# Row-wise scores for one head in four of ten groups, in an attention and Fourier kernel

## The chip, the cores and the metric

The kernel runs on one core of one Trainium2 chip. TensorE (PE) multiplies matrices into PSUM, VectorE (DVE), ScalarE (ACT) and GpSimd (POOL) work on tiles, and SyncE (SP) issues nearly all DMAs, in order, one queue for all of them. The metric is the time of one execution in microseconds on the device. Times are given as the median of several runs; the profile is of one further execution.

## The reference

Two independent parts stand side by side in the output. Part A is an attention with a compressive memory: 2,048 positions, 32 heads of 18 features, in four segments of 512 positions. In each segment a causal softmax attention runs within the segment; from the second segment on it is blended with a lookup in a memory that sums the keys and values of the segments before. Part B is a Fourier mixing layer: two products with DFT matrices, of which the real part is kept.

```python
for s in range(4):
    logits = einsum("bhqd,bhkd->bhqk", qs, ks) * 18 ** -0.5 + causal_mask
    a_dot = einsum("bhqk,bhkd->bhqd", softmax(logits), vs)
    a_mem = (phi(qs) @ M) / (phi(qs) @ z + 1e-6)
    o[s] = g * a_mem + (1 - g) * a_dot
    M, z = M + phi(ks).T @ vs, z + phi(ks).sum()
A = concat(o) @ wo
B = dft_seq_re @ (x @ dft_hid_re.T) - dft_seq_im @ (x @ dft_hid_im.T)
```

All of it is float32, and the kernel keeps its precision by splitting numbers into a high and a low part (or three bfloat16 parts) and adding the products.

## The kernel before

It has three stages. In the first (to some 220 us) the projections are computed segment by segment. Queries and keys go to DRAM scratch (`qd`, `kd`) in three bfloat16 parts each, values (`vd`, [128, 4 position blocks, 8 groups, 220]) and the finished memory lookups (`amd`, [4, 128, 576]) too. In the second, the attention of all heads and the Fourier products run interleaved. The third, short one multiplies by `wo`.

The change lies in the second stage. Its units:

- A group G is four heads of one segment; there are 32 groups, 8 for each segment. Head n is head h = n % 4 of group n // 4. `stack_load(G)` loads the group's `ks` and `qs`, `value_load(G)` its values `vst`, `memory_load(G)` its lookups into `og` (from G = 8 on).
- A phase p handles pairs of heads, an even one and the odd one next to it, at several lags, so a head passes through several phases. A phase has eight slots with nominal widths (`SLOTS`). After each slot the generator `attention` yields, DMAs and work put off by `later` are issued, and dense Fourier matmuls (`d`) are dealt out until their share of the nominal total is reached. All order is written out in this way; every engine executes its instructions in that order.
- All 512 x 512 scores of a head, in the causal lower half, are 1,280 columns of PE work: row block i (128 queries) needs (i + 1) x 128 keys.

An odd head is formed by rows. `f_fill` (kinds 0, 1, 2) multiplies the rows' scores into PSUM (`scores`, L958), and DVE masks the diagonal block and takes each row's minimum of the negated score in one pass (`smallest`, L964). `f_exp` takes the exponential on ACT with that minimum as bias (L984, L987), into `pf`. `f_split_hi` (ACT, L994) and `f_split_lo` (POOL for 768 columns, DVE for 512, L998) split it into two float16 halves `hl`. `f_turn` (L1003) transposes `hl` by a DMA into `ptt`, as `pv` needs keys on the partitions. That is lag 2 for the scores, lag 3 for split and turn, lag 4 for `pv`, which multiplies by the values (L1076, L1077).

An even head is formed transposed, without a DMA transpose. `s_fill` scores the rows at lag 0 only for their minima (`NEGM`). For both even heads of a group, `maxima` (POOL) cuts the minima into three bfloat16 parts, `maxima_transpose` turns them on PE (L1015) and two small DMAs (L1019) put them under `qs` as three more rows. At lag 3 `t_fill` computes the transposed scores with the minima folded in (seven matmuls, L1032 to L1041), and ACT takes exponentials into the high half `phi` and the full `pf` (L1044, L1045). `t_mask` zeroes the upper triangle of the diagonal blocks (POOL, L1049), `t_hi` copies (ACT, L1054), and `t_lo` makes `plo` (DVE and POOL, L1059).

PSUM has two banks for `s` tiles and two for `t` tiles, taken in turns. `pf` is a ring of three tiles; `phi`, `plo`, `hl` and `ptt` are rings of two. The dense part loads chunks `craw` four ahead (`c_load`, L441); `c_cut` splits a chunk on ACT (`chi`, L451) and POOL (`clo`, L456).

Of the kernel before, what the change touches and what calls it, by code (L numbers as in the profile page):

```python
# [23 lines left out]
P = 128  # L24
# [10 lines left out]

COPIES = ((0, 3, 2, 0), (1, 3, 2, 2), (0, 5, 1, 0), (1, 5, 1, 1))
COPY_ROWS = 144


@with_exitstack  # L40
def infini_attention_and_fnet(ctx: ExitStack, tc: tile.TileContext, xT, wqk, w8, wv, wo, beta, xtT, cT, hT, out):
# [10 lines left out]
    vd = [dram.tile([P, 4, 8, 220], BF16, name=f"vd{s}") for s in range(NSEG)]  # L52
    amd = [dram.tile([4, P, D], F32, name=f"amd{s}") for s in range(NSEG)]
# [255 lines left out]
    def project_v(s, j, meanwhile):  # L309
        xh, xl, xt = X[s]  # L310
        js = slice(j * P, (j + 1) * P)
        vs = vs_bufs[(4 * s + j) % 3]
        r = sb.tile([P, H, DH], F32, name="vr", tag="r", bufs=3)
        for h in range(2):
            cs, hs = slice(h * 288, (h + 1) * 288), slice(16 * h, 16 * h + 16)
            o = ps.tile([P, 288], F32, name="v", tag="acc", bufs=5)
            terms = []
            for k in range(4):
                terms += [(xh[k][:, js], WV[1][k][:, cs]), (xh[k][:, js], WV[0][k][:, cs]),
                          (xl[k][:, js], WV[0][k][:, cs])]  # L320
            terms += [(xt[:, js], WV[2][:, cs]), (xt[:, js], WV[3][:, cs])]
            chain(o, terms)
            o = o.rearrange("p (h d) -> p h d", d=DH)
            act.activation(vs[:, hs, 18:36], o, AF.Copy)
            if s < 3:
                split(vn[j % 2][:, 0, hs, :DH], vn[j % 2][:, 1, hs, :DH], o)
            dve.tensor_tensor(r[:, hs], o, vs[:, hs, 18:36], OP.subtract)
            if h == 0 and s < 3:
                k_natural(j)
            next(meanwhile, None)  # L330
        if s < 3 and j == 3:
            for k in range(2, 5):
# [4 lines left out]
        later(1, dma, vd[s][:, j], vs.rearrange("p (g h) c -> p g (h c)", g=8))  # L337

    started = set()

# [49 lines left out]
    def lookup(s, j):  # L390
        js = slice(j * P, (j + 1) * P)
        nd = sb.tile([P, H, 19], F32, name="nd", bufs=2)
        o = ps.tile([P, 3, 8, 19], F32, name="look", tag="acc", bufs=5)
        for c in range(3):
            for n, (a, half) in enumerate(((pq_hi, 1), (pq_hi, 0), (pq_lo, 0))):
                pe.matmul(o[:, c], a[:, c, js], md[:, c, half], start=c + n == 0, stop=True, skip_group_check=True)
        act.activation(nd[:, :21].rearrange("p (c h) e -> p c h e", c=3), o[:, :, :7], AF.Copy)
        yield

        u = ps.tile([P, L], F32, name="look", tag="acc", bufs=5)  # L400
        u3, u4 = (u[:, at:at + 2 * n].rearrange("p (k h e) -> p k h e", k=2, e=19) for at, n in ((0, 152), (304, 76)))
# [16 lines left out]
        later(1, dma, amd[s][j], am.rearrange("p h d -> p (h d)"))  # L418
        yield

    HW, HRAW = {}, {}
# [71 lines left out]

    def value_load(G):
        if G < NG:
            s, g8 = divmod(G, 8)
            VS[G] = sa.tile([P, 4, 220], BF16, name="vst", bufs=2)
            dma(VS[G], vd[s][:, :, g8])

    for s in range(NSEG):  # L500
        more = s < 3
# [194 lines left out]
    def right_operands():  # L696
# [108 lines left out]
        for t, tag in ((1, "phi"), (9, "plo")):  # L805
            at(67, 4, o_load, t, lambda tag=tag: sa.tile([P, 5, P], F32, name="oraw", tag=tag, bufs=2))
        at(67, 4, lambda: list(left(0)))

    def left(n):
# [161 lines left out]
    F_ = {}  # L971

    def f_fill(n, kind):
        o = scores(n, kind, "s" if kind else "t")
        if kind == 1:
            F_[n] = [sa.tile([P, 4], F32, name="nb", bufs=2), sa.tile([P, 1280], F32, name="pf", bufs=3), {}]
        smallest(o, kind, -SCALE, F_[n][0])
        F_[n][2][kind] = o
# [9 lines left out]

    def f_split_hi(n):
        f = F_[n][1]  # L990
        hl = sa.tile([P, 2, 1280], F16, name="hl", bufs=2)
        F_[n][2] = hl
        for a, b in ((512, 1280), (0, 512)):
            act.activation(hl[:, 0, a:b], f[:, a:b], AF.Copy)  # L994
# [4 lines left out]

    def f_turn(n):  # L1000
        hl = F_.pop(n)[2]
        PT[n] = sa.tile([P, 20, P], F16, name="ptt", bufs=2)
        nc.sync.dma_start_transpose(PT[n], hl.rearrange("p a c -> p (a c)"))  # L1003

    def maxima(G):
# [7 lines left out]
    def maxima_transpose(G, o):  # L1013
# [2 lines left out]
        w = sa.tile([24, P], BF16, name="mt", bufs=2)  # L1016
        act.activation(w, t[:24], AF.Copy)
        for h in range(2):
            later(1, dma, qs_bufs[G % 4][NPAIR:NPAIR + 3, 2 * h].rearrange("c (n t) -> c n t", n=4), w[12 * h:12 * h + 12])  # L1019

    def t_fill(n, kind, maxima_of=None):
        G, h = divmod(n, 4)
        q, k = qs_bufs[G % 4][:NPAIR + 3, h], ks_bufs[G % 4][:NPAIR + 3, h]
        if kind == 0:
            PT[n] = (sa.tile([P, 1280], F16, name="phi", bufs=2), sa.tile([P, 1280], F16, name="plo", bufs=2),
                     sa.tile([P, 1280], F32, name="pf", bufs=3))
        hi, lo, f = PT[n]
        o = bank("t", [P, L], F32, "t")
        if kind == 0:
# [31 lines left out]
    def pv(n):  # L1061
# [4 lines left out]
        for i in range(4):  # L1066
            o = PV[n // 2][:, (h % 2 * 4 + i) * 55:(h % 2 * 4 + i + 1) * 55]
            for j in range(i + 1):
                if h % 2:
# [59 lines left out]
    def memory_load(G):  # L1129
        if 8 <= G < NG:  # L1130
            s, g8 = divmod(G, 8)
            dma(OG[G % 2], amd[s][:, :, 72 * g8:72 * g8 + 72].rearrange("q p c -> p q c"))

    F_LAG, T_LAG, V_LAG = 2, 3, 4
    NP = 2 * NG
# [2 lines left out]
    def attention():  # L1138
        for p in range(NP + V_LAG):
            def even(lag, fn, *a):  # L1140
                if 0 <= p - lag < NP:
                    fn(2 * (p - lag), *a)

            def odd(lag, fn, *a):
                if 0 <= p - lag < NP:
# [11 lines left out]
            even(T_LAG + 1, t_lo, 0)  # L1157
# [4 lines left out]
            even(0, s_fill, 0)  # L1162
            even(T_LAG, t_fill, 0)
            even(T_LAG, t_fill, 1, G)
# [4 lines left out]
            even(0, s_fill, 1)  # L1169
            odd(F_LAG + 1, f_split_lo, dve, 0, 512)  # L1170
            yield SLOTS[2]
            even(V_LAG, pv)
            even(0, s_fill, 2)
            even(T_LAG, t_mask)
            yield SLOTS[3]
            odd(F_LAG, f_fill, 1)
            even(T_LAG, t_fill, 2)
# [11 lines left out]
            even(T_LAG, t_hi)  # L1189
# [4 lines left out]
            even(T_LAG, t_lo, 1)  # L1194
            even(T_LAG, t_lo, 2)
            yield SLOTS[6]
            odd(F_LAG, f_exp, 0)
            if V_LAG <= p < NP + V_LAG - 1:
# [77 lines left out]
```

## Time and profile before

| | us |
|---|---|
| median of 3 runs | 993.25 (992.81 to 993.87) |
| profiled execution | 994.13 |
| its span, first to last instruction | 992.4 |

One line of the page has the DMA queues; SP's queue, q1, is nearly all of it:

```profile
q1 hardware_dynamic: 304000, 208.20, 80.9%
```

It gives the packets, the megabytes, and the time that the packets took as a share of sixteen DMA engines over the span. In groups of instructions a row reads: line, engine, operation, result<-operands with shapes, count | busy time, mean ns of one | idle time just before them. In a timeline a row is start, duration, engine, line, operation. Matmuls are pipelined, so the distance between two starts tells what one costs, not its own duration. Rows of SP are DMA issues; what they last is SP's time, not the transfer's.

### The profile page before, as it was taken

How to read it: one execution, taken by the hardware profiler on the slowest of the kernel's cores; microseconds unless marked ns; L12 is line 12 of the kernel's file. 1: busy time of each engine (PE TensorE's matmuls, PEld its weight loads, DVE VectorE, ACT ScalarE, POOL GpSimd, SP SyncE). 2: the span in 40 equal slices, each digit the busy share in tenths (PEclk: the TensorE clock that was granted, in tenths of full speed). 3: DMA queues.
4: the chain of work that ended last, by engine and by line, in shares of the span. 5: the costliest groups of instructions: out<-in, count | busy, mean ns of one | idle time of the engine just before them, and what ended most of it. 6: DMA issues, size and time to landing. Idle time of an engine off the chain costs nothing.

```text
span 992.4 us, 25495 instructions
## 1 busy us (share of the span) xinstructions
PE 980.9 (99%) x9246; PEld 918.3 (93%) x9246; DVE 786.4 (79%) x2115; ACT 714.7 (72%) x1687; POOL 675.2 (68%) x744
## 2 busy tenths in 40 slices
PE   9999999999999999999999999999999999999998
PEld 8988989898999999999999999999999999999998
DVE  6657668584678787887898878888888898989985
ACT  6757576563888777877878788886777778788442
POOL 2657576686676667676775777767676667887561
PEclk9999999999999999999999999999999999999999
DMA  7537556777578898899999998779999999988663
GB/s 241 191 117 244 194 170 241 238 243 214 146 179 206 224 239 227 203 226 241 223 253 242 235 211 191 187 196 218 247 231 219 224 241 252 249 200 180 168 199 112
DMA packets 304351, 209.97 MB, mean 212 GB/s; under 512 B 204992, under 2 KB 259136, under 8 KB 304192
## 3 DMA queue, kind: packets, MB, share of 16 engines
q1 hardware_dynamic: 304000, 208.20, 80.9%
q8 instruction: 72, 1.18, 0.5%
q14 instruction: 55, 0.45, 0.1%
q10 hardware_dynamic: 224, 0.14, 0.0%
HBM read 122.37 MB, written 58.98 MB: 183 GB/s over the span
## 4 chain that ended last, share of the span: by engine, by line
PE 84%; DVE 7%; ACT 4%; DMA 2%; issue 2%; POOL 1%; SPq 0%; POOLq 0%; DVEq 0%; ACTq 0%
PE d L583 38%; PE s L958 7%; PE v L84 4%; PE pv L1076 4%; PE qk L250 4%; PE d L628 3%; PE d L629 3%; PE d L630 3%; PE t L861 2%; PE pv L1077 2%; PE m L363 1%; PE d L861 1%; PE s L861 1%; PE t L1032 1%; PE qk L84 1%
## 5 line engine op out<-in xcount | busy, mean ns | idle before, releaser
L964 DVE CUSTOM_DVE_ANT_0 s<-s,causal 128x128 f32<-128x128 f32 (+3 forms) x512 | 248.4, 503 | 94.2 <-PE s L958 85.0
L456 POOL TENSOR_TENSOR clo<-craw,chi 128x512 fp32r<-128x512 f32 x158 | 218.2, 1381 | 91.1 <-ACT chi L451 60.8
L583 PE MATMUL d<-wide,chi 128*128 128x288 f32 x1408 | 261.9, 303 | 0.2 <-DVE y L653 0.2
L583 PEld LDWEIGHTS d<-wide,chi 128*128 128x128 f32 x1408 | 210.6, 188 | 2.7 <-issue 0.7
L583 PE MATMUL d<-wide,clo 128*128 128x288 f32 x704 | 173.4, 313 | 0.0
L998 POOL TENSOR_TENSOR hl<-pf,hl 128x768 f16<-128x768 f32 x64 | 114.0, 1782 | 67.4 <-ACT hl L994 55.6
L958 PE MATMUL s<-ks,qs 108*128 108x128 bf16 (+3 forms) x512 | 132.9, 303 | 1.7 <-DVE negm L964 1.2
L1044 ACT ACTIVATE phi<-t 128x384 f16<-128x384 f32 x128 | 61.8, 483 | 100.1 <-PE t L1041 100.1
L987 ACT ACTIVATE pf<-s,nb 128x128 f32<-128x128 f32 (+3 forms) x256 | 128.3, 527 | 6.2
L583 PE MATMUL d<-ab,chi 128*128 128x288 f32 x640 | 123.3, 302 | 0.0
L1059 DVE TENSOR_TENSOR plo<-pf,phi 128x384 f16<-128x384 f32 (+1 forms) x128 | 122.3, 955 | 0.0
L583 PEld LDWEIGHTS d<-wide,clo 128*128 128x128 f32 x704 | 117.8, 189 | 1.4
L1045 ACT ACTIVATE pf<-t 128x384 f32<-128x384 f32 (+1 forms) x192 | 99.6, 519 | 6.6 <-PE t L1032 6.3
L451 ACT ACTIVATE chi<-craw 128x512 fp32r<-128x512 f32 x160 | 100.1, 626 | 4.0 <-DMA craw<-xtT 2.4
L583 PEld LDWEIGHTS d<-ab,chi 128*128 128x128 f32 x640 | 97.8, 188 | 0.5
L994 ACT ACTIVATE hl<-pf 128x768 f16<-128x768 f32 (+1 forms) x128 | 87.4, 729 | 2.0
L583 PE MATMUL d<-ab,clo 128*128 128x288 f32 x320 | 83.0, 308 | 0.0
L628 PE MATMUL d<-wide,chi 128*128 128x288 f32 x256 | 81.4, 318 | 0.0
L630 PE MATMUL d<-wide,clo 128*128 128x288 f32 x256 | 75.6, 296 | 0.9 <-POOL clo L456 0.9
L629 PE MATMUL d<-wide,chi 128*128 128x288 f32 x256 | 75.6, 295 | 0.0
L1059 POOL TENSOR_TENSOR plo<-pf,phi 128x384 f16<-128x384 f32 x64 | 61.7, 963 | 12.0 <-ACT pf L1045 9.1
L998 DVE TENSOR_TENSOR hl<-pf,hl 128x512 f16<-128x512 f32 x64 | 69.2, 1081 | 0.0
(285 smaller groups left out, 2521.9 us busy)
## 6 DMA issues: line engine op xcount, KB each, us to landing
craw<-cT SPq DMA_DIRECT2D x128, 256.0 KB
ks<-kd SPq DMA_DIRECT2D x32, 432.0 KB
qs<-qd SPq DMA_DIRECT2D x32, 432.0 KB
craw<-xtT SPq DMA_DIRECT2D x32, 320.0 KB
vd<-vs SPq DMA_DIRECT2D x16, 440.0 KB
vst<-vd SPq DMA_DIRECT2D x32, 220.0 KB
qd<-p SPq DMA_DIRECT2D x16, 384.0 KB
kd<-p SPq DMA_DIRECT2D x16, 384.0 KB
```

The lines of the kernel that those rows point to most:

```text
L451: act.activation(hi, raw[:, :4], AF.Copy)
L456: engine.tensor_tensor(lo, raw[:, :4], hi.bitcast(F32), OP.subtract)
L583: pe.matmul(o[h], a, b[:, h * 288:h * 288 + 288], start=start, stop=stop)
L628: pe.matmul(o, xh[:, k], wl[k][:, cs], start=k == 0, stop=False)
L629: pe.matmul(o, xh[:, k], wh[k][:, cs], start=False, stop=False)
L630: pe.matmul(o, xl[:, k], wh[k][:, cs], start=False, stop=False)
L958: pe.matmul(o[:, c:c + w], q[:, i * P:w], k[:, :w], start=True, stop=True)
L964: dve.tensor_tensor_reduce(o[:, c:c + w], o[:, c:c + w], CAUSAL[0][:, L - w:], scale=scale, scalar=-LOWEST, op0=OP.add, op1=OP.min, accum_ ...
L987: act.activation(f[:, FIRST_COL[i]:FIRST_COL[i] + w], o[:, c:c + w], AF.Exp, bias=nb[:, i:i + 1], scale=-1.0)
L998: engine.tensor_tensor(hl[:, 1, a:b], f[:, a:b], hl[:, 0, a:b], OP.subtract)
L1045: act.activation(f[:, r:r + w], o[:, :w], AF.Exp, bias=LIFT, scale=SCALE)
L1059: (pool if kind == 2 else dve).tensor_tensor(lo[:, a:b], f[:, a:b], hi[:, a:b], OP.subtract)
```

## The change

For ten heads, listed in `ROWWISE` (the first head of groups 2 to 7 and of groups 16 to 19), the transposed forming is replaced by the row-wise one. Such a head has no `s_fill`, `t_fill`, `t_mask`, `t_hi`, `t_lo` and no `mt` load. Instead, at lag 3, it goes through `f_fill` in the order 0, 1, 2 (slots 0, 1, 3), all of it in the `t` banks, `f_exp` one slot behind each, `f_split_hi` at slot 4, `f_split_lo` at slot 5 and `f_turn` at slot 6; `pv` comes one phase later at slot 5. As these heads are the first of their groups, all of this falls in odd phases, p = 2G + 3. In those phases `stack_load` of the next group is put off by two slots, behind the new turn.

Tiles: `phi` and `plo` become one ring `phl` of two; a row-wise head's `ptt` comes from `phl`, and its halves (`hle`) from the `pf` ring. Two loads late in the kernel that used `phi` and `plo` now share one `phl` tile. In segments 0 to 2 the scratch `vd` is [128, 8, 4, 220] and `amd` is [128, 8, 4, 72], so that a group's load reads one run for each partition and a store writes eight.

```diff
+ROWWISE = (8, 12, 16, 20, 24, 28, 64, 68, 72, 76)
...
+    vd = [dram.tile([P, 8, 4, 220] if s < 3 else [P, 4, 8, 220], BF16, name=f"vd{s}") for s in range(NSEG)]
+    amd = [dram.tile([P, 8, 4, 72] if s < 3 else [4, P, D], F32, name=f"amd{s}") for s in range(NSEG)]
...
     def f_fill(n, kind):
-        o = scores(n, kind, "s" if kind else "t")
-        if kind == 1:
+        o = scores(n, kind, "s" if kind and n % 2 else "t")
+        if n not in F_:
...
-        hl = sa.tile([P, 2, 1280], F16, name="hl", bufs=2)
+        hl = (sa.tile([P, 2, 1280], F16, name="hl", bufs=2) if n % 2
+              else sa.tile([P, 2, 1280], F16, name="hle", tag="pf", bufs=3))
...
-        PT[n] = sa.tile([P, 20, P], F16, name="ptt", bufs=2)
+        PT[n] = sa.tile([P, 20, P], F16, name="ptt", tag="ptt" if n % 2 else "phl", bufs=2)
...
         for h in range(2):
+            if 4 * G + 2 * h in ROWWISE:
+                continue
...
-            PT[n] = (sa.tile([P, 1280], F16, name="phi", bufs=2), sa.tile([P, 1280], F16, name="plo", bufs=2),
-                     sa.tile([P, 1280], F32, name="pf", bufs=3))
+            t = sa.tile([P, 2, 1280], F16, name="phl", bufs=2)
+            PT[n] = t[:, 0], t[:, 1], sa.tile([P, 1280], F32, name="pf", bufs=3)
...
+            rowwise(T_LAG, f_fill, 0)
             yield SLOTS[0]
+            rowwise(T_LAG, f_fill, 1)
...
+            rowwise(T_LAG, f_exp, 0)
             yield SLOTS[1]
...
+            rowwise(T_LAG, f_exp, 1)
             yield SLOTS[2]
...
+            rowwise(T_LAG, f_fill, 2)
             yield SLOTS[3]
...
+            rowwise(T_LAG, f_exp, 2)
+            rowwise(T_LAG, f_split_hi)
             yield SLOTS[4]
             odd(F_LAG + 1, f_turn)
             if p % 2:
-                stack_load((p + 3) // 2)
+                if 2 * (p - T_LAG) in ROWWISE:
+                    later(2, stack_load, (p + 3) // 2)
+                else:
+                    stack_load((p + 3) // 2)
...
+            rowwise(T_LAG, f_split_lo, pool, 512, 1280)
+            rowwise(T_LAG, f_split_lo, dve, 0, 512)
             yield SLOTS[5]
+            rowwise(V_LAG, pv)
             odd(V_LAG, pv)
...
+            rowwise(T_LAG, f_turn)
             yield SLOTS[6]
```

The calls of `even` for `s_fill`, `t_fill`, `t_mask`, `t_hi`, `t_lo` and the first `pv` become calls of `turned`, which leaves the ten heads out.

More of the change, by code (lines that the diff above doesn't have):

```diff
@@ L51, in infini_attention_and_fnet @@
     kd = [dram.tile([D, 6, L], BF16, name=f"kd{s}") for s in range(NSEG)]
-    vd = [dram.tile([P, 4, 8, 220], BF16, name=f"vd{s}") for s in range(NSEG)]
-    amd = [dram.tile([4, P, D], F32, name=f"amd{s}") for s in range(NSEG)]
+    vd = [dram.tile([P, 8, 4, 220] if s < 3 else [P, 4, 8, 220], BF16, name=f"vd{s}") for s in range(NSEG)]
+    amd = [dram.tile([P, 8, 4, 72] if s < 3 else [4, P, D], F32, name=f"amd{s}") for s in range(NSEG)]
     yd = [dram.tile([P, D], F32, name=f"yd{t}") for t in range(NT)]
@@ L336, in project_v @@
         pool.tensor_tensor(vs[:, :, 0:18], r, vs[:, :, 36:54], OP.subtract)
-        later(1, dma, vd[s][:, j], vs.rearrange("p (g h) c -> p g (h c)", g=8))
+        later(1, dma, vd[s][:, :, j] if s < 3 else vd[s][:, j], vs.rearrange("p (g h) c -> p g (h c)", g=8))
     started = set()
@@ L417, in lookup @@
         pool.tensor_tensor(am, nd[:, :, :DH], w.to_broadcast([P, H, DH]), OP.mult)
-        later(1, dma, amd[s][j], am.rearrange("p h d -> p (h d)"))
+        if s < 3:
+            later(1, dma, amd[s][:, :, j], am.rearrange("p (g h) d -> p g (h d)", g=8))
+        else:
+            later(1, dma, amd[s][j], am.rearrange("p h d -> p (h d)"))
         yield
@@ L497, in value_load @@
             VS[G] = sa.tile([P, 4, 220], BF16, name="vst", bufs=2)
-            dma(VS[G], vd[s][:, :, g8])
+            dma(VS[G], vd[s][:, g8] if s < 3 else vd[s][:, :, g8])
     for s in range(NSEG):
@@ L804, in right_operands, with second @@
                 "p a x -> p (a x)")[:, :5 * P].rearrange("p (k x) -> p k x", k=5))
-        for t, tag in ((1, "phi"), (9, "plo")):
-            at(67, 4, o_load, t, lambda tag=tag: sa.tile([P, 5, P], F32, name="oraw", tag=tag, bufs=2))
+        both = []
+        def second():
+            both.append(sa.tile([P, 2, 5, P], F32, name="oraw", tag="phl", bufs=2))
+            for i in range(2):
+                o_load(1 + 8 * i, lambda: both[0][:, i])
+        at(67, 4, second)
         at(67, 4, lambda: list(left(0)))
@@ L1068, in pv @@
             for j in range(i + 1):
-                if h % 2:
+                if h % 2 or n in ROWWISE:
                     b = FIRST_COL[i] // P + j
@@ L1131, in memory_load @@
             s, g8 = divmod(G, 8)
-            dma(OG[G % 2], amd[s][:, :, 72 * g8:72 * g8 + 72].rearrange("q p c -> p q c"))
+            dma(OG[G % 2], amd[s][:, g8] if s < 3 else amd[s][:, :, 72 * g8:72 * g8 + 72].rearrange("q p c -> p q c"))
     F_LAG, T_LAG, V_LAG = 2, 3, 4
@@ L1142, in even, with turned, rowwise @@
                     fn(2 * (p - lag), *a)
+            def turned(lag, fn, *a):
+                if 2 * (p - lag) not in ROWWISE:
+                    even(lag, fn, *a)
+            def rowwise(lag, fn, *a):
+                if 2 * (p - lag) in ROWWISE:
+                    even(lag, fn, *a)
             def odd(lag, fn, *a):
@@ L1156, in attention @@
                 later(30, memory_load, p // 2)
-            even(T_LAG + 1, t_lo, 0)
+            turned(T_LAG + 1, t_lo, 0)
             odd(F_LAG + 1, f_exp, 2)
             odd(F_LAG + 1, f_split_hi)
+            rowwise(T_LAG, f_fill, 0)
             yield SLOTS[0]
+            rowwise(T_LAG, f_fill, 1)
             G = p // 2 - 1 if p % 2 == 0 and 0 < p <= NP else None
-            even(0, s_fill, 0)
-            even(T_LAG, t_fill, 0)
-            even(T_LAG, t_fill, 1, G)
+            turned(0, s_fill, 0)
+            turned(T_LAG, t_fill, 0)
+            turned(T_LAG, t_fill, 1, G)
             if G is not None and p < T_LAG:
@@ L1167, in attention @@
             odd(F_LAG + 1, f_split_lo, pool, 512, 1280)
+            rowwise(T_LAG, f_exp, 0)
             yield SLOTS[1]
-            even(0, s_fill, 1)
+            turned(0, s_fill, 1)
             odd(F_LAG + 1, f_split_lo, dve, 0, 512)
+            rowwise(T_LAG, f_exp, 1)
             yield SLOTS[2]
-            even(V_LAG, pv)
-            even(0, s_fill, 2)
-            even(T_LAG, t_mask)
+            turned(V_LAG, pv)
+            turned(0, s_fill, 2)
+            turned(T_LAG, t_mask)
+            rowwise(T_LAG, f_fill, 2)
             yield SLOTS[3]
             odd(F_LAG, f_fill, 1)
-            even(T_LAG, t_fill, 2)
+            turned(T_LAG, t_fill, 2)
             odd(F_LAG, f_fill, 0)
@@ L1188, in attention @@
                 later(2, copy_parts, 3, (p - 4) // 2)
-            even(T_LAG, t_hi)
+            turned(T_LAG, t_hi)
+            rowwise(T_LAG, f_split_lo, pool, 512, 1280)
+            rowwise(T_LAG, f_split_lo, dve, 0, 512)
             yield SLOTS[5]
+            rowwise(V_LAG, pv)
             odd(V_LAG, pv)
@@ L1193, in attention @@
             odd(F_LAG, f_exp, 1)
-            even(T_LAG, t_lo, 1)
-            even(T_LAG, t_lo, 2)
+            turned(T_LAG, t_lo, 1)
+            turned(T_LAG, t_lo, 2)
+            rowwise(T_LAG, f_turn)
             yield SLOTS[6]
```

1 line of the change is left out of this document (added).

## The prediction

> **What bounds the kernel now.** I read the page's busy times first, then what TensorE (PE) waits for during attention, then the windows of the stretches in which the ten changed heads run.
>
> ```profile
> span 992.4 us, 25495 instructions
> PE 980.9 (99%) x9246; PEld 918.3 (93%) x9246; DVE 786.4 (79%) x2115; ACT 714.7 (72%) x1687; POOL 675.2 (68%) x744
> ```
> ```profile
> PE pv L1077 <- DVE plo L1059: 0.4, 1, 0.4
> PE s L958 <- DVE negm L964: 0.4, 1, 0.4
> PE d L583 <- DVE y L653: 0.2, 1, 0.2
> ```
> ```profile
> 0.00:220.00 220.00, 218.51 (x1331) 197.47 (x1332) 147.74 (x310) 145.73 (x327) 139.90 (x152) 1.00 0.63 209
> 420.00:560.00 140.00, 139.95 (x1519) 131.27 (x1518) 120.35 (x350) 113.25 (x267) 99.14 (x108) 1.00 0.99 236
> 305.25:416.84 111.59, 111.59 (x1221) 104.97 (x1220) 89.31 (x265) 88.53 (x210) 78.61 (x89) 1.00 0.89 224
> 592.35:673.76 81.41, 81.03 (x850) 76.65 (x849) 67.57 (x206) 65.22 (x163) 59.71 (x71) 1.00 0.80 192
> ```
>
> The middle block is every wait of PE between 245 and 920 us: three, 1.0 us together. In the windows (columns: length, then busy time of PE, its weight loads, DVE, ACT and POOL, granted clock, DMA share, GB/s) PE is busy 111.59 of 111.59 us. So PE's own work sets the end at full clock, DVE, ACT and POOL run behind it with a sixth or more free on average, and the one other resource near its end is DMA. What PE no longer computes comes off the time, unless something new makes it wait. The third window runs from the turn of phase 7 to that of phase 18, eleven phases of 10.14 us; it holds the row-wise work of six of the ten heads (phases 7, 9, ... 17). The fourth does so for the other four (phases 35 to 41), seven phases of 11.63 us.
>
> **The change on PE.** An even head is scored twice now: `s_fill` for the row minima (four matmuls, 1,280 columns in all) and `t_fill` for the transposed scores (seven matmuls, again 1,280 columns). A row-wise head is scored once, by `f_fill`, with four matmuls and 1,280 columns. The `pv` matmuls keep their count. What columns cost is read from the starts in PE's timeline, since a matmul's own time overlaps its neighbour's:
>
> ```profile
> 330.98 0.39 PE L958 MATMUL s<-ks,qs 108*128 108x512 bf16 x1
> 331.20 0.39 PE L1032 MATMUL t<-qs,ks 111*128 111x128 bf16 x4
> 331.43 0.33 PE L1035 MATMUL t<-qs,ks 111*128 111x384 bf16 x1
> 331.59 0.22 PE L1015 MATMUL t<-ident,mb 128*128 128x128 bf16 x1
> ...
> 335.20 0.22 PE L1040 MATMUL t<-qs,ks 111*128 111x128 bf16 x1
> 335.26 0.27 PE L1041 MATMUL t<-qs,ks 111*128 111x256 bf16 x1
> 335.37 0.38 PE L958 MATMUL s<-ks,qs 108*128 108x512 bf16 x1
> ```
>
> The head's own `t` matmuls take 0.23 + 0.16 + 0.06 + 0.11 = 0.56 us for 1,280 columns, and the 512 columns of `s` take 0.22, the same rate. So one scoring is worth 0.56 us; replacing `t_fill` by `f_fill` is even, dropping `s_fill` saves 0.56, and ten heads save 5.6 us. L1015 stays, since the group's second even head still needs its minima. The dense matmuls are dealt out by nominal slot weights that the change leaves alone, so none of them moves to another phase.
>
> **DVE.** The row-wise work falls in the odd phases, three phases after the head's place, the dropped `s_fill` in even ones. Prices in the third window:
>
> ```profile
> L964 DVE CUSTOM_DVE_ANT_0 s<-s,causal 128x512 f32<-128x512 f32 x22 | 15.7, 712 | 1.2 <-PE s L958 1.1
> L998 DVE TENSOR_TENSOR hl<-pf,hl 128x512 f16<-128x512 f32 x12 | 14.4, 1199 | 0.0
> L964 DVE CUSTOM_DVE_ANT_0 s<-s,causal 128x384 f32<-128x384 f32 x22 | 12.5, 566 | 0.8
> L1059 DVE TENSOR_TENSOR plo<-pf,phi 128x512 f16<-128x512 f32 x11 | 10.7, 971 | 0.0
> L964 DVE CUSTOM_DVE_ANT_0 s<-s,causal 128x256 f32<-128x256 f32 x23 | 9.8, 428 | 9.8 <-PE s L958 9.7
> L1059 DVE TENSOR_TENSOR plo<-pf,phi 128x384 f16<-128x384 f32 x11 | 8.8, 803 | 0.0
> L964 DVE CUSTOM_DVE_ANT_0 s<-s,causal 128x128 f32<-128x128 f32 x22 | 6.8, 308 | 9.5 <-PE s L958 8.5 <-ACT pf L1045 0.9
> ```
>
> Four minima are 0.71 + 0.57 + 0.43 + 0.31 = 2.0 us. An odd phase gains these and a 512-wide low part (1.2) and loses one 384-wide low part (0.8): +2.4 on a mean of 89.31/11 = 8.1, so 10.5 us in a phase of 10.1. An even phase loses 2.0 and the 512-wide `plo` of 0.97 and falls to 5.1. Over the pair DVE is lighter by 0.6 us, but in the odd half it is overdrawn by 0.4 and must finish in the light half. What is queued behind the new low part on DVE is the minimum of the odd head's last fill and the `pv` evacuation; PE waits for them only when it needs that PSUM bank again, a slot or more later. I bound the loss between nothing and the whole saving, 0.56 per head, and take 0.1 per head, near the lower end, because DVE waited 19 us for PE's scores in the last two 128 and 256 rows above, so it usually is ahead. Sum: +1.0 us.
>
> ```profile
> L987 ACT ACTIVATE pf<-s,nb 128x128 f32<-128x128 f32 (+3 forms) x256 | 128.3, 527 | 6.2
> L1045 ACT ACTIVATE pf<-t 128x384 f32<-128x384 f32 (+1 forms) x192 | 99.6, 519 | 6.6 <-PE t L1032 6.3
> L994 ACT ACTIVATE hl<-pf 128x768 f16<-128x768 f32 (+1 forms) x128 | 87.4, 729 | 2.0
> ```
>
> ACT exchanges five exponentials and a copy (5 x 0.52 + 0.73 = 3.3 us by these rows) for four exponentials, two copies (4 x 0.53 + 2 x 0.73 = 3.6) and three bias copies of one column, each between nothing and an exponential's 0.53: 0.3 to 1.9 us more in an odd phase. I take 1, as they are far smaller than an exponential; 88.53/11 = 8.0 plus 1 fits into 10.1. POOL gives up mask and a 384-wide low part and takes a 768-wide low part, about even. Both at nothing; without that cover ACT's microsecond would stand in the odd phases, 10 us in all.
>
> **DMA and the SP queue.** Each row-wise head adds one DMA transpose of 128 x 2,560 two-byte elements, 655 KB, and drops one small `mt` load.
>
> ```profile
> 346.40:349.40 3.00, 3.00 (x41) 2.93 (x40) 2.93 (x10) 2.80 (x9) 1.93 (x6) 1.00 1.14 213
> 316.43:325.64 9.21, 9.21 (x106) 8.63 (x105) 7.49 (x21) 6.72 (x17) 6.02 (x5) 1.00 0.97 257
> ```
> ```profile
> L1003 SPq DMA_TRANSPOSE ptt<-hl x64: 3037/3745/6270, 258.7 to 918.4; - x64
> ```
> ```profile
> 325.64 3.09 SPq L1003 DMA_TRANSPOSE ptt<-hl  x1
> 328.78 0.54 SPq L94 DMA_DIRECT2D ks<-kd  x1
> ...
> 330.50 0.53 SPq L441 DMA_DIRECT2D craw<-cT  x1
> ...
> 332.92 1.60 SPq L94 DMA_DIRECT2D qs<-mt  x2
> 334.62 0.37 SPq L441 DMA_DIRECT2D craw<-cT  x1
> 335.16 3.71 SPq L1003 DMA_TRANSPOSE ptt<-hl  x1
> ...
> 339.54 0.62 SPq L498 DMA_DIRECT2D vst<-vd  x1
> ```
>
> Little but a transpose moves between 346.4 and 349.4 us, at 213 GB/s, so one takes 655/213 = 3.1 us of all queues, at a share of 1.14 (packets overlap) 3.5 us of share. A pair of phases lasts 20.3 us; 3.5/20.3 lifts 0.89 to 1.06, and the rate from 224 to 256 GB/s. A phase with 257 GB/s stands above, with PE busy throughout, so I take no loss; the bound on the other side is the DMA rival below. The Trainium skill, DMA: Bandwidth & Descriptors, section Latency and other measured facts, gives a DMA transpose 261 GB/s, or 350 to 400 where contiguous; this trace has 213, and by the page's 261 the added share would be nearer 0.14 than 0.17, with the sum as it is.
>
> On SP the instruction itself blocks the queue for 3.0 to 6.3 us, median 3.7. In phase 9 (325.64 is its turn) the new transpose comes straight behind the old one, once its low parts are done. Queued behind it are the next group's `ks` and `qs` loads (their first reader comes three phases later, 30 us, so nothing), the copies between scratch rows, `craw` at 330.50, the remaining `mt` load and the next turn at 335.16. The instructions of SP from the one turn to the next leave 1.8 of 9.5 us free; with 3.7 more, less 0.8 for the `mt` load dropped (two take 1.60), the next turn goes out 1 us late, or 2 where the new transpose has to wait for its low parts, and the even phase, with one transpose, catches up. Late next are `craw` and the transposed head itself:
>
> ```profile
> 341.36 0.62 ACT L451 ACTIVATE chi<-craw 128x512 fp32r<-128x512 f32 x1
> ```
> ```profile
> 337.98 0.20 PE L1076 MATMUL pv<-vst,ptt 128*128 128x55 bf16 x1
> ```
>
> The tile asked for at 330.50 is read at 341.36, 10.9 us later; issued 3.4 us late behind 3.1 us more data it still has some 2 us, if those add at most to 9. The old turn of 325.64 is read by `pv` at 337.98; a row-wise head is read in the same slot. Its turn, estimated 3.3 us behind the old one, has 9 us left for 3.1 us of data and the wait before it. So both are covered, `craw` thinly: uncovered, each missed microsecond would stop ACT, then PE.
>
> **Scratch by group and tiles.** A `vst` or `og` load now reads one run for each partition instead of four, and its store writes eight instead of one. A load's 0.62 us on SP can only fall (gain at most 0.6 each, hidden behind PE); the twelve `vd` and eight `amd` stores grow, but go out in the first 220 us, where the DMA share is 0.63. At nothing. The shared tile rings (`phl`, and `hle` from `pf`) release each buffer at least half a phase before its next writer, by the order of the statements. Nothing too.
>
> **Sum.** 994.13 us of the profiled execution (992.4 span, 1.7 around it) - 5.6 + 1.0 = 989.5. The median of the three runs lies 0.9 lower, 993.25, so the forecast is 988.6 us.
>
> **Rivals.**
>
> DVE becomes the bound of the odd phases. For it: 10.5 us of work in 10.1. Then an odd phase lasts 10.5 to 10.7 and the pair keeps its 20.3 us, so the saving is eaten: 993.3. Against it: the pair as a whole is lighter on DVE. Chance 0.13.
>
> DVE and POOL collide on the new head's two low parts, which start together and sit in front of the next minimum on DVE.
>
> ```profile
> L998 POOL TENSOR_TENSOR hl<-pf,hl x64: 1646/1664/2166, 256.4 to 914.4; 128x768 f16<-128x768 f32 x64
> L998 DVE TENSOR_TENSOR hl<-pf,hl x64: 679/859/2136, 257.1 to 916.5; 128x512 f16<-128x512 f32 x64
> ```
>
> At 2.1 us instead of 1.2 the odd phase has 11.4 us of DVE, 0.9 more than in the rival before: 993.3 + 10 x 0.9 = 1002. The same instruction does spread from 0.68 to 2.14 us beside POOL's; but its median is 0.86. Chance 0.07. The Trainium skill, SBUF — State Buffer, section SBUF: two separate sides, says that a VectorE operation with two SBUF inputs and a GpSimd operation that reads SBUF lock each other out for a whole instruction; the spread agrees with that.
>
> DMA sets the pace in groups 2 to 7; this one ends slower. If 0.99, the highest share held over a long stage above, is what the queues can carry, a pair there needs (0.89 x 20.3 + 3.5)/0.99 = 21.8 us, 1.5 more than now, six times: +9; the four heads at 0.80 fit (0.95) and save 2.2. That gives 1000. It decides from a share of about 1.04 on, where 21.1 us of queue work meet 20.3. For it: two transposes back to back and a thin `craw`. Against it: 1.14 and 257 GB/s are both on record without a wait of PE. Chance 0.15.
>
> That PE's work doesn't shrink can't be: the changed program has 70 matmuls fewer.
>
> **How the numbers follow.** The forecast has 0.65; its own range is 986.8 to 991. The whole range goes from 986.8 (all 5.6 saved, nothing given back, and the spread of the runs) to 996.5, past the first rival and into part of the DMA case (a loss half its size); left out are most of the two that end at 1000 and more. This kernel's runs tell about 0.2%, 2 us, from no change. Faster by more: 0.65 (0.62 from the forecast, 0.03 from a milder DVE case); within: 0.11; slower: 0.24.
>
> **What would show it.** PE's `s` and `t` matmuls 40 and 70 fewer, 40 new ones in their place, and PE waits in attention of 1 to 3 us: right. DVE 0.5 us busier in its odd phases than their length, with PE waiting for DVE or ACT at L958's successor: the first or second rival. ACT waiting for `craw` at the `chi` line, or PE for `ptt` at `pv`, and phases 7 to 18 longer than 10.14 us: DMA. The forecast is wrong if phases 4 to 18, which drop six `s_fill`, don't shrink by about 3 us.

## The result and the profile after

The changed kernel takes 1006.33 us (median of 4 runs, 1003.52 to 1010.82) beside 993.56 us for the kernel before (992.81 to 996.03), a ratio of 1.0131 with a 95% interval of 1.0113 to 1.0148: slower by 13 us, where 988.6 was forecast. The profiled execution took 1005.36 us.

The page of the changed kernel, busy times and SP's queue (q1):

```profile
span 1003.6 us, 25404 instructions
PE 981.5 (98%) x9176; PEld 917.8 (91%) x9176; DVE 787.4 (78%) x2105; ACT 723.7 (72%) x1717; POOL 670.4 (67%) x734
...
q1 hardware_dynamic: 332330, 214.72, 86.8%
```

PE issues 70 matmuls fewer, yet is busy as long, since some of it ran at a lower clock. The phases tell where the time went. The mark of a phase is DVE's reciprocal of `pv_out`, late in the phase:

| stretch | before, us | after, us |
|---|---|---|
| start to phase 4 | 275.4 | 275.6 |
| 4 to 10 | 64.2 | 63.7 |
| 10 to 18 | 80.9 | 89.6 |
| 18 to 32 | 143.6 | 144.4 |
| 32 to 44 | 133.8 | 134.3 |
| 44 to 66 | 222.7 | 222.7 |
| 66 to the end | 71.7 | 73.2 |

Of the 11 us between the two profiled spans 8.7 are lost in phases 10 to 18, with four of the ten heads. The phases of the first two heads (4 to 10) gain 0.5 us, half of what was forecast for them, and those of the four late ones (32 to 44) nothing. The windows of phases 10 to 18 (length, busy PE, weight loads, DVE, ACT, POOL, clock, DMA share, GB/s), of before and of after:

```profile
339.60:420.50 80.90, 80.90 (x886) 76.01 (x886) 65.32 (x194) 63.99 (x152) 56.94 (x62) 1.00 0.88 220
```
```profile
339.30:428.90 89.60, 83.11 (x862) 77.19 (x861) 65.82 (x206) 69.30 (x167) 55.54 (x58) 0.96 1.05 234
345.00:350.00 5.00, 3.93 (x34) 3.46 (x34) 2.93 (x11) 4.75 (x13) 3.75 (x7) 0.67 0.97 244
370.60:374.00 3.40, 3.40 (x15) 2.99 (x15) 2.03 (x7) 3.21 (x7) 1.94 (x2) 0.50 0.94 250
```

PE stands 6.5 of 89.6 us and has two stretches of 3.4 us at half clock, each worth 1.7 us. Priced by what PE executes there (0.43 ns a score column, 0.134 us a dense matmul, 0.027 us one of `pv`), its work fell by 1.6 us and the clock took 3.4; the 6.9 us that are left of the 8.7 are idle time, of which the trace shows 6.5 as gaps.

What PE and ACT wait for in the changed kernel (245 to 920 us for PE, 300 to 442 us for ACT):

```profile
PE s L968 <- ACT pf L997: 4.4, 4, 2.6
PE pv L1089 <- DMA ptt<-hle: 2.3, 2, 1.3
PE t L1045 <- DMA qs<-mt: 1.6, 1, 1.6
PE s L968 <- DVE negm L974: 1.1, 3, 0.8
...
ACT chi L455 <- DMA craw<-cT: 6.7, 3, 3.2
```
```profile
344.10 0.63 ACT L455 ACTIVATE chi<-craw 128x512 fp32r<-128x512 f32 x1 [2.71 <-DMA craw<-cT]
```

PE's largest wait is for ACT's exponential, and ACT had stood 2.71 us in front of a `chi` that waits for `craw`. The queue in front of that load, SP's timeline (start, duration):

```profile
326.54 4.25 SPq L1014 DMA_TRANSPOSE ptt<-hl  x1
330.89 3.56 SPq L1014 DMA_TRANSPOSE ptt<-hle  x1
...
337.27 0.45 SPq L445 DMA_DIRECT2D craw<-cT  x1
...
338.29 0.80 SPq L95 DMA_DIRECT2D qs<-mt  x1
...
339.74 5.92 SPq L1014 DMA_TRANSPOSE ptt<-hl  x1
...
348.59 4.77 SPq L1014 DMA_TRANSPOSE ptt<-hl  x1
353.47 3.10 SPq L1014 DMA_TRANSPOSE ptt<-hle  x1
```

The `craw` issued at 330.50 before goes out at 337.27, 6.8 us later, lands at 344.02 and is read 0.08 us after. The turn after it lasts 5.92 us instead of 3.71. All turns in phases 10 to 18 (count: shortest/median/longest, ns), before and after:

```profile
L1003 SPq DMA_TRANSPOSE ptt<-hl x8: 3101/3512/3673, 345.1 to 416.8; - x8
```
```profile
L1014 SPq DMA_TRANSPOSE ptt<-hl x9: 4111/4769/6644, 339.7 to 428.4; - x9
L1014 SPq DMA_TRANSPOSE ptt<-hle x4: 3105/3399/3702, 353.5 to 421.4; - x4
```

So SP doesn't only hold the four new turns, 3.4 us each; the odd heads' turns also grew by 1.3 us. Summed over SP's DMA issues, as far as they lie between the two marks, SP is taken for 14.7 us per pair of phases before (20.2 us long) and for 20.8 us after (22.4 long). In phases 4 to 10 of the changed kernel, which lose nothing, it is 16.4 of 21.2.

### The profile page after: what moved, and what is told of

It is laid out like the page before. It is cut to its first block, busy times and chain, and to the rows that moved or that the text cites. A ratio compares the mean times of both kernels' runs of the same rounds, so it can differ in the third digit from the quotient of the medians.

```text
span 1003.6 us, 25404 instructions
## 1 busy us (share of the span) xinstructions
PE 981.5 (98%) x9176; PEld 917.8 (91%) x9176; DVE 787.4 (78%) x2105; ACT 723.7 (72%) x1717; POOL 670.4 (67%) x734
## 4 chain that ended last, share of the span: by engine, by line
PE 70%; DVE 9%; ACT 7%; DMA 5%; issue 4%; POOL 3%; SPq 1%; POOLq 0%; DVEq 0%; ACTq 0%
PE d L587 30%; PE s L968 6%; PE pv L1089 3%; PE qk L251 3%; PE v L85 3%; PE d L632 3%; PE d L634 3%; PE d L633 3%; PE t L871 2%; PE pv L1090 2%; PE s L871 1%; DMA craw<-cT 1%; PE d L871 1%; POOL clo L460 1%; DMA raw<-xT 1%
## 5 line engine op out<-in xcount | busy, mean ns | idle before, releaser
L997 ACT ACTIVATE pf<-s,nb 128x384 f32<-128x384 f32 (+3 forms) x296 | 148.1, 526 | 9.5 <-DMA ptt<-hle 1.7
L968 PE MATMUL s<-ks,qs 108*128 108x128 bf16 (+3 forms) x512 | 129.5, 304 | 7.2 <-ACT pf L997 4.4
L1057 ACT ACTIVATE phl<-t 128x384 f16<-128x384 f32 x108 | 51.8, 480 | 72.8 <-PE t L1054 72.8
L1072 DVE TENSOR_TENSOR phl<-pf,phl 128x384 f16<-128x384 f32 x108 | 104.0, 963 | 0.0
L1058 ACT ACTIVATE pf<-t 128x512 f32<-128x512 f32 x162 | 83.8, 517 | 7.2 <-PE t L1045 7.1
L1009 DVE TENSOR_TENSOR hl<-pf,hl 128x512 f16<-128x512 f32 x64 | 73.0, 1140 | 11.3 <-ACT hl L1005 11.3
L994 ACT ACTIVATE nb<-nb 128x1 f32<-128x1 f32 (+1 forms) x222 | 44.0, 198 | 22.3 <-DVE nb L974 21.8
```

What stands on the lines that cost most here:

```text
L968: pe.matmul(o[:, c:c + w], q[:, i * P:w], k[:, :w], start=True, stop=True)
L997: act.activation(f[:, FIRST_COL[i]:FIRST_COL[i] + w], o[:, c:c + w], AF.Exp, bias=nb[:, i:i + 1], scale=-1.0)
L1009: engine.tensor_tensor(hl[:, 1, a:b], f[:, a:b], hl[:, 0, a:b], OP.subtract)
L1072: (pool if kind == 2 else dve).tensor_tensor(lo[:, a:b], f[:, a:b], hi[:, a:b], OP.subtract)
```

## The experiments

Theory: the new transposes fill SP's in-order queue in groups 2 to 7; what stands behind them (`craw`, `mt`, the next turn) goes out late, ACT and PE stand, and pauses of PE bring half-clock stretches. Rivals: their bytes load the DMA queues; the engines' row-wise work makes the waits; the scratch layout costs it.

| run | ratio to before | 95% interval |
|---|---|---|
| layout_only | 1.0021 | 1.0011 to 1.0031 |
| rows_only | 1.0083 | 1.0061 to 1.0104 |
| small_turn | 1.0008 | 0.9995 to 1.0021 |
| rows_small | 0.9979 | 0.9969 to 0.9989 |
| dead_turns | 1.0081 | 1.0064 to 1.0098 |
| dead_copies | 0.9997 | 0.9984 to 1.0010 |
| dead_tiny | 1.0011 | 1.0000 to 1.0023 |
| dead_both | 1.0042 | 1.0026 to 1.0058 |
| turns_deep | 1.0073 | 1.0052 to 1.0095 |
| rows_deep | 1.0096 | 1.0067 to 1.0124 |
| craw_on_act | 1.0219 | 1.0162 to 1.0275 |
| loads_ahead | 1.0100 | 1.0085 to 1.0115 |
| spaced | 1.0002 | 0.9991 to 1.0014 |
| late_four | 0.9994 | 0.9983 to 1.0005 |
| rows_relieved | 1.0737 | 1.0707 to 1.0767 |
| before_relieved | 1.0331 | 1.0315 to 1.0346 |
| rows_pool | 1.1447 | 1.1423 to 1.1470 |
| before_pool | 1.1069 | 1.1022 to 1.1116 |

Small differences below are these ratios, in us of 994.

**The two parts by themselves: the layout (layout_only) and the row-wise heads with the old layout (rows_only).**

> The kernel before with the scratch laid out by group and nothing else. The prediction put this at nothing: 993.5 +- 0.5 us. Rival (the stores in eight short runs hold up the loads of x behind them): PE stands some 1.7 us for qk near 63 us, as in the profile of the changed kernel, and the time is 995 to 996.

> The changed kernel with the old scratch layout. Queue theory (the added transposes delay the dense chunk loads): most of the loss stays, 1003 to 1006. If the layout were the main cause: 988 to 991.

The layout alone costs 2.1 us, the heads alone 8.3. The layout's profiled execution shows its phases 0.3 us later throughout and 1.8 us more behind phase 66, 1.7 of it one half-clock stretch at 939.4 us; other executions with the old layout have this stretch too (rows_only at 946.9 us, dead_turns at 945.8), so where the layout's 2 us of the medians arise is not shown.

**The transposes taken out (small_turn, and rows_small with the old layout).** The row-wise heads turn 2 of their 20 blocks, and `pv` multiplies by these two.

```diff
-        nc.sync.dma_start_transpose(PT[n], hl.rearrange("p a c -> p (a c)"))
+        if n % 2:
+            nc.sync.dma_start_transpose(PT[n], hl.rearrange("p a c -> p (a c)"))
+        else:
+            nc.sync.dma_start_transpose(PT[n][:, :2], hl[:, 0, :2 * P])
...
-                    hi, lo = pt[:, b], pt[:, 10 + b]
+                    hi, lo = (pt[:, b], pt[:, 10 + b]) if h % 2 else (pt[:, 0], pt[:, 1])
```

> The changed kernel, in which the ten row-wise heads transpose only 2 of 20 blocks, and their pv uses those two blocks throughout; all of PE's, DVE's, ACT's and POOL's work stays. Queue theory: the waits of ACT for craw go away, time 988 to 991 (993.5 - 5.6, and up to 2 for the layout). Engine theory (DVE and ACT overdrawn in the odd phases, or the low parts colliding): stays at 1002 to 1006.

> The changed kernel with the old scratch layout and with the row-wise heads' transpose cut to 2 of 20 blocks (18 of 20 blocks of those heads are left out; pv multiplies by the two): what the change is worth without the layout and without the transposes. If the sum of the prediction held apart from its DMA step and the layout: 989 (5.6 saved, 1.0 given back). If engine waits eat most of it, as the run with the new layout and the small transposes suggests: 991 to 992.5.

With the new layout 994.18 us, which neither theory had (988 to 991, or 1002 to 1006). With the old layout 992.14 us: by the ratio 2.1 us under before. Against rows_only the transposes' size is worth 1.0083 - 0.9979, 10 us, more than the whole loss. PE's largest wait left (rows_small, 245 to 920 us) is for the minima on DVE:

```profile
PE s L965 <- DVE negm L971: 2.2, 4, 1.1
PE s L965 <- ACT pf L1058: 0.4, 1, 0.4
```

**The transposes put in alone (dead_turns).** The kernel before, with transposes of 18 of the odd head's 20 blocks at the ten places, into tiles that nothing reads.

```diff
+    def dead():
+        for i in range(2):
+            t = sb.tile([P, 9, P], F16, name="dead", tag="raw", bufs=3)
+            nc.sync.dma_start_transpose(t, LASTHL[0][:, i, :9 * P])
...
             even(T_LAG, t_lo, 2)
+            if 2 * (p - T_LAG) in ROWWISE:
+                dead()
```

> The kernel before, unchanged in its computing, with the ten added transposes alone: in the same phases, at slot 6, the odd head's halves are transposed once more into tiles that nothing reads (two transposes of 9 blocks each, 18 of the 20 blocks). Queue theory: the loss appears without any row-wise head, +7 to +11 us, 1001 to 1005, with ACT waiting for craw. Engine theory: 993 to 995.

1001.97 us. No engine computes anything new here, and a loss as large as that of rows_only is there: 8.1 us, four fifths of the 10 that the transposes are worth among row-wise heads. PE's and ACT's largest waits on loads (245 to 920 and 300 to 442 us) are for loads that stand behind the turns, PE's for `mt`:

```profile
PE t L1034 <- DMA qs<-mt: 6.0, 4, 2.0
...
ACT chi L452 <- DMA craw<-cT: 9.1, 3, 4.7
```

**Their bytes alone, SP's time alone, and both (dead_copies, dead_tiny, dead_both).** At the same places: one copy of 655 KB from DRAM to DRAM (0.54 us of SP); five copies of 3 KB (3.3 us of SP); one large and four small.

```diff
+        DEAD.append(dram.tile([P, 5, L], BF16, name=f"dead{len(DEAD)}"))
+        dma(DEAD[-1], qd[0][:P, :5])
...
+        for i in range(5):
+            DEAD.append(dram.tile([3, 4, P], BF16, name=f"dead{len(DEAD)}"))
+            dma(DEAD[-1], qd[0][:3, 0].rearrange("c (n t) -> c n t", n=4))
```

> The kernel before with ten added plain copies of 655 KB from scratch to unused scratch at the same places, so that the DMA engines get as many bytes while SP is held only for one plain issue of about 0.5 us. If the DMA engines' time is what runs out: +5 us or more, 999 or above. If SP standing for some 4 us in the transpose instruction is the cause: within 1 us of before, 993 to 995.

> The kernel before, with five tiny copies (3 x 512 bfloat16, 3 KB each, DRAM to DRAM) put into SP's queue at each of the ten places of the added transposes: about 4 us of SP time a place, next to no bytes. If the loss comes from SP's time alone, SP is held as long as by a transpose: 998 to 1002, with ACT standing at chi for craw. If it needs what a transpose does beside that (its own turns getting longer, its bytes, its transfers in the rings): 993 to 995, within 0.15% of before.

> The kernel before, with at each of the ten places one 655 KB copy from DRAM to DRAM and four tiny ones (3 KB each): a transpose's bytes and about a transpose's time on SP, without a transpose. The bytes alone cost nothing, SP's time alone about 1 us. If the two only matter together (issued late, and landing late): 998 to 1002, as with the dead transposes. If it is something that only a transpose does in the rings: 994 to 996.

The bytes alone cost nothing, SP's time alone 1 us, both together 4.2 us: more than their sum, as expected if the two matter together, and about half of what the transposes cost. Windows of phases 10 to 18 of dead_copies, dead_both and dead_turns:

```profile
338.40:420.00 81.60, 81.09 (x886) 76.03 (x886) 65.69 (x194) 63.84 (x152) 56.91 (x62) 1.00 1.04 251
```
```profile
338.30:423.90 85.60, 82.07 (x886) 76.07 (x885) 65.65 (x194) 64.27 (x152) 56.87 (x62) 1.00 0.95 243
```
```profile
338.80:426.80 88.00, 83.54 (x886) 77.33 (x885) 64.67 (x195) 64.25 (x152) 56.46 (x62) 0.98 1.03 233
```

A DMA share of 1.04 at 251 GB/s goes with a PE that stands 0.5 us; a share of 0.95 with one that stands 3.5. The share doesn't order the runs. SP's time does, summed as above over phases 10 to 18, per pair of phases:

| run | SP, us per pair | length of the pair, us |
|---|---|---|
| before | 14.7 | 20.2 |
| dead_copies | 17.3 | 20.4 |
| rows_small | 17.4 | 20.1 |
| spaced | 18.2 | 20.7 |
| dead_tiny | 18.7 | 20.5 |
| dead_both | 19.1 | 21.4 |
| rows_deep | 20.2 | 21.6 |
| turns_deep | 20.3 | 21.8 |
| dead_turns | 20.4 | 22.0 |
| changed kernel | 20.8 | 22.4 |
| rows_only | 21.2 | 22.7 |

Up to 18.7 us of SP the pair of 20.2 us loses at most 0.5; from 19.1 on it is longer by 1.2 us or more. SP's time holds what its turns wait in being issued, so it is a measure of the crowding as well as its cause, and of runs so near each other as the last five the order says nothing.

**One of the late loads brought forward (turns_deep, rows_deep).** `craw` asked for earlier, from the same four buffers, in dead_turns and in rows_only:

```diff
         c_load(n + 4)
+        later(1, c_load, n + 5)
```

> The kernel before with the ten dead transposes (1,002 us), and each craw load issued one chunk less one slot earlier (the same four buffers). If the loss comes through craw being late (ACT stands at chi, the pauses bring half-clock stretches): most of the 8 us go, 994 to 997, no half-clock stretch. If a late mt load or the slots of the rings do it: 1000 to 1003.

> The changed kernel with the old scratch layout (1,002.6 us), and each craw load issued one chunk less one slot earlier. If craw is the way of the loss: 994 to 997 (992 without any loss from the transposes); what is left over then is pv waiting for the row-wise head. If not: 1001 or more.

Both expectations of a recovery failed. The time from the issue of a `craw` to its reading, 10.8 us before in the mean of phases 10 to 18, was nearly restored (7.0 in dead_turns, 9.9 in turns_deep), but PE stood for others behind the turns. Its wait for `mt`, 4.0 us in phases 10 to 18 of dead_turns, is in turns_deep:

```profile
PE t L1035 <- DMA qs<-mt: 4.9, 4, 1.7
PE pv L1079 <- DMA ptt<-hl: 0.6, 1, 0.6
```

In rows_deep PE stood for the row-wise heads' own turns, 3.4 us in these phases (4.5 in rows_only). `craw` is one place where the lateness shows, not its cause: more than one load behind the turns is late.

**The place of loads in the queue (loads_ahead, craw_on_act).** loads_ahead is the changed kernel with `stack_load((p + 3) // 2)` where it was before, not behind the new turn. craw_on_act issues `craw` from ACT:

```diff
-            dma(t[:, :k], src[at])
+            nc.scalar.dma_start(t[:, :k], src[at])
```

> The changed kernel with the next group's row loads issued where they were, ahead of the new transpose. Queue theory: the row-wise head's own transpose and the chunk loads then stand behind 0.9 MB more in the rings, PE waits longer for it at pv: same or worse, 1006 to 1012. If putting the loads behind was itself the harm: 1000 or less.

> The changed kernel with the dense chunk loads issued on ACT's queue instead of SP's; the transposes stay whole. If the loads are late because they stand behind the transposes in SP's order and its rings: no wait of ACT for craw in phases 7 to 18, 990 to 995. If the transposes take too much of the DMA engines' time wherever the loads are issued: 1000 or more. Engine theory: 1002 to 1006.

loads_ahead is 1003.65 us, not above the changed kernel (1.0100 beside 1.0131), against the expected 1006 to 1012: putting the loads off brings nothing. craw_on_act removed every wait of ACT for `craw<-cT` and lost more, since the turns themselves grew (to 8.7 us) and PE stood for them (245 to 920 us):

```profile
PE pv L1089 <- DMA ptt<-hl: 11.5, 6, 3.4
PE pv L1089 <- DMA ptt<-hle: 4.0, 2, 2.7
PE s L968 <- DVE negm L974: 2.7, 3, 1.6
```

Its time is also what was expected if the transfers take too much of the DMA engines' time (1000 or more), so it doesn't decide between the two. In the turn of 8.7 us packets of other transfers were moving for 8.6.

**Other issues taken off SP (rows_relieved and rows_pool, controls before_relieved and before_pool).** The scratch copies and the group's loads issued from ACT (with the `mt` loads) or from POOL:

```diff
-        dma(x[:, to:to + parts], a)
+        (act.dma_start if started_attention else dma)(x[:, to:to + parts], a)
```

> The changed kernel with the old scratch layout, and with the mt loads, the copies between scratch rows and the loads of the next group issued from ACT's queue in the second stage instead of SP's: about 20 us of SP time less in groups 2 to 7. If SP's queue is the cause, most of the 9 us over before go: 989 to 995, no ACT wait for craw over 1 us. Against it: as in the run that moved craw to ACT, an issue on ACT waits for earlier transfers to land and ACT's exponentials stand behind it: 1000 or more, with PE waiting for ACT or for ptt.

> Control: the kernel before with the same loads and copies issued from ACT's queue. If ACT's issues are cheap where the rings aren't backlogged: 993 to 995. If they hold up ACT by themselves: 998 or more, and then the run with the row-wise heads can't speak against SP's queue.

> The changed kernel with the old scratch layout (1,002.6 us), and with the copies between scratch rows and the loads of the next group issued by POOL in the second stage instead of SP: 12.7 us of SP's 105 in the window 305 to 417 us go, with the same transposes and the same bytes. If SP's in-order queue is what is short: 992 to 997, PE waiting less than 2 us for ptt or mt. If the transposes' transfers in the DMA rings are what is short, whoever issues the rest: 1000 or more, with SP's transposes as long as before (5 us). If POOL, held by its own issues, becomes late: PE or ACT waiting for POOL.

> Control: the kernel before with the same loads and copies issued by POOL. If these issues cost POOL nothing that PE needs: 992.5 to 995. If 997 or more, the run with the row-wise heads is read against this one, not against before.

The controls lose 33 and 109 us by themselves, so these four don't decide for or against SP. With these issues among its instructions ACT stood until transposes had landed, rows_relieved in 245 to 440 us:

```profile
ACT pf L996 <- DMA ptt<-hle: 14.4, 3, 6.1
...
ACT chi L454 <- DMA ptt<-hle: 9.3, 1, 9.3
ACT phl L1056 <- DMA ptt<-hle: 8.5, 1, 8.5
```

**Fewer heads (spaced, late_four; old layout).** `ROWWISE = (8, 16, 24, 64, 72)` and `ROWWISE = (64, 68, 72, 76)`.

> Old scratch layout, row-wise heads only in groups 2, 4, 6 and 16, 18 (five instead of ten, never in two odd phases running). Queue theory: the share that a transpose adds is spread over four phases, craw catches up in between, no half-clock stretch in phases 4 to 18: 991 to 994 (5 x 0.56 saved, up to half of it lost to DVE and ACT waits). If each row-wise head costs the same wherever it stands: half the loss, 997 to 999.

> The change for the four late heads alone (groups 16 to 19), with the old scratch layout. By the prediction's sum, 0.56 - 0.1 for each of four heads: 991.5. By the phases of the changed kernel, where these four give back 1.7 of 2.2 us to engine waits: 993 to 993.5, not told from before.

Neither differs from before by what can be told. That spaced, with five of the ten heads, loses nothing, where half the loss (997 to 999) was expected if each head had its price, fits a queue that overflows only when the turns come close together. In late_four's phases 34 to 42 SP is taken for 19.9 us, but a pair there lasts 23.3 us, and PE has no DMA wait. Of all versions that do the whole computation none is faster than before.

## Why the prediction was wrong

**The step that failed is "DMA and the SP queue"**, taken at no loss: "the next turn goes out 1 us late, or 2 where the new transpose has to wait for its low parts, and the even phase, with one transpose, catches up". It added one turn (3.7 us) and took off one `mt` load. On the 14.7 us of a pair that makes 17.6 of 20.2, which fits, and dead_tiny, at 18.7, shows that such a load is carried for about 1 us. What was not priced is that the other turns don't keep their 3.5 us: their median rose to 4.77, and SP came to 20.8 us. Then the even phase has little left to catch up in (from 322.5 to 361.5 us SP's issues follow each other with no gap over 0.2 us), and `craw`, covered "thinly" with "some 2 us", was 6.8 us late instead of 3.4 and had nothing. The phases the prediction named as its test, 4 to 18, grew by 8.2 us instead of shrinking by 3.

**The DMA rival** named the right place (groups 2 to 7), signs and size (1000 us), with 0.15. Its price, a share of 0.99 that the queues can carry, is wrong: dead_copies runs at 1.04 through phases 10 to 18 in 81.6 us beside 80.9, and its median is that of before. What fills is SP's queue of instructions; bytes come into it by the way told below.

**PE's saving** is right in its mechanism: one scoring less for each head, and without transposes and layout the kernel is faster. Its net size is off: 2.1 us in rows_small where 5.6 - 1.0 was forecast. **The DVE term** was the one mis-sized. In rows_small's phases 4 to 18 and 32 to 44 PE's idle time rose by 3.6 us by the prices above (2.5 of it show as gaps), 0.36 per head instead of 0.1, inside the bounds of 0 and 0.56, and the largest wait is for a minimum on DVE, though for one of an even head (`negm`). late_four has 0.36 too. So even a free transpose would have left a third of the saving. The first rival on DVE, which has the whole 0.56 eaten, lay no further off than the value taken, but no run shows DVE as the bound.

**The layout** at nothing was wrong by some 2 us. The sum from runs is 10.3 (transposes) + 2.1 (layout) - 2.1 (heads without either) = 10.3 of the 13 us; the other 2.7 are not assigned: the changed kernel lies further above rows_only than the layout alone accounts for, and half-clock stretches vary from execution to execution.

**Why a turn lengthens** the traces' DMA packets tell in part. A turn moves 2,560 packets of 256 bytes. In the kernel before, the turn issued at 345.11 us had nothing ahead of it; in the changed kernel that of 339.74 had loads ahead (windows as above, DMA share and GB/s last):

```profile
345.10:346.10 1.00, 1.00 (x13) 0.88 (x10) 0.74 (x4) 0.39 (x2) 1.00 (x2) 1.00 0.00 0
```
```profile
339.74:342.20 2.46, 2.46 (x21) 2.22 (x20) 2.40 (x7) 1.61 (x3) 1.26 (x1) 1.00 0.96 308
342.20:344.20 2.00, 2.00 (x31) 1.93 (x30) 1.93 (x8) 0.10 (x1) 0.64 (x1) 1.00 1.81 245
344.20:345.20 1.00, 0.32 (x9) 0.15 (x6) 1.00 (x4) 0.97 (x3) 0.34 (x1) 1.00 0.27 32
```

The first held SP for 3.10 us. The second held it for 5.92: for 5.1 of them packets larger than its own (440 bytes and more, 1.14 MB) were still moving, and it let go 0.8 us after the last of these. In the changed kernel the six turns with no such packets beside them took 3.0 to 3.2 us, the 42 with over 500 KB a median of 4.5, and the five longest in phases 10 to 18 all ended 0.8 us after the last packet of an earlier transfer. So a lengthened turn keeps SP until what was issued ahead of it has drained. That fits both lengthenings: bytes with little SP time (dead_copies, median 4.4 us) put more ahead of a turn, and SP time with hardly any bytes (dead_tiny, 4.3) brings the turn closer behind its loads. It is read from the times alone; no run varies only what lies ahead of a turn.

**What stays open** is the half of the transposes' cost that dead_both doesn't show. Its SP is taken for 19.1 us a pair and that of dead_turns for 20.4, but whether this is all of the difference no run tells. Its copies move from DRAM to DRAM, so a cost that only a transpose has isn't excluded.

## What to carry to other kernels

Sum the time of the issuing queue over a whole period, turns included, as one sums an engine's. Here 18.7 us of 20.2 were carried and 19.1 were not, so past about nine tenths of the period an added transfer is to be priced as a loss. Price the neighbours' turns by what is still moving when they are issued, at their upper spread, not at their median: at the median the sum here was 17.6 and looked safe. A thin reserve on one load can show the fullness of the whole queue: bringing that load forward left the waits for the others. When dropping work on the bounding engine moves work to others, measure that half without the transfer first; here it was worth 2 us of 5.6.

## What the runs showed of the hardware

PE's clock fell to half for 3.4 us after shorter pauses. A row of the changed kernel's timeline:

```profile
369.25 0.27 PE L968 MATMUL s<-ks,qs 108*128 108x256 bf16 x1 [2.57 <-ACT pf L997]
```

After this pause of 2.57 us the clock was 0.50 from 370.6 to 374.0 (window above). The pause in front of the stretch at 346.7 us was 1.07 and 0.47 us with a few matmuls between. The Trainium skill, TensorE: Matmul & The Clock Gate, section What's actually happening, gives the low state after at least one idle window of about 3.4 us, with windows that run freely; the length of the stretch agrees, but here shorter pauses were enough. Whether one does it varies: the same pause late in the kernel brought a stretch in the changed kernel's execution (1.87 us, stretch at 947.4 us) and none in that of before (1.91 us).

A transpose of 655 KB held SP for 3.0 to 9.5 us in these runs (9.5 in rows_relieved), plain issues for 0.4 to 0.6, a copy of 3 KB on 3 partitions for 0.62. Some 150 ordinary loads and copies cost 33 us when ACT issued them, and 109 us when POOL issued all of these but the `mt` loads.
